# A new order of steps for a two-stage attention and token-mixing kernel, with batches 2 and 3 mixed in three pieces

## The chip, the cores and the metric

The kernel runs on one core of one Trainium2 chip. The metric is the time of one execution on the device in microseconds. The engines are named as the profile names them: PE (TensorE, the matmuls), PEld (its weight loads), DVE (VectorE), ACT (ScalarE), POOL (GpSimd) and SP (SyncE, used here only to issue DMAs). ACT and POOL can issue DMAs too.

## What is computed

Inputs q, k, v are of shape 8 batches x 8 heads x 576 tokens x 64, p is 8 x 8 x 32 x 64, all float32. The reference packs the tokens into 32 by an attention of p over k and v, and unpacks them by an attention of q over the packed tokens. The result, with heads side by side, is x (8 x 576 x 512), and goes through a mixing of tokens that is linear up to a relu:

```python
def sm_attn(qq, kk, vv):
    s = scale * np.matmul(qq, kk.transpose(0, 1, 3, 2))
    s = s - np.max(s, axis=-1, keepdims=True)
    a = np.exp(s)
    a = a / (np.sum(a, axis=-1, keepdims=True) + 1e-09)
    return np.matmul(a, vv)
p_packed = sm_attn(p, k, v)
out = sm_attn(q, p_packed, p_packed)
...
wq = x @ w_q
wk = x @ w_k
W_tok = scale * np.einsum('bsd,btd->bst', wq, wk)
mixed = np.einsum('bst,btd->bsd', W_tok, x)
return (np.maximum(mixed, 0.0) @ w_out).astype(np.float32)
```

## The kernel before

The work is cut by batch. Each batch b goes through the same steps, and each step is a small function whose name stands in a long string, ORDER. The loop at the end of the kernel walks through ORDER and emits one step after another, in a mode in which nothing reorders them: so ORDER is, for each engine and each DMA queue, the order of its work. Waits between engines follow from the data and the buffers. An item reads `NAME.batch.piece=banks@engine`; the banks are the PSUM banks that a matmul step writes, A, V, P and S are ACT, DVE, POOL and SP.

The steps of one batch, with the line at which the work is recorded where that isn't a shared helper:

- LD (loads). k, q and v come in over the POOL queue, and are cast from float32 to bf16 on the way; two halves of the batch's heads are two transfers for v always. In this kernel k is one transfer per batch (576 KB in bf16 counted as the profile does), but batch 0, whose first half comes as float32 over SP (LD.H, cast by HC) and whose second half is LD.g0. q is one transfer, but for batches 0 and 7 (LD.q and LD.r are its halves). LD.W, LD.O are weights, LD.P and LD.E parts of p. The order of LD items is the order in the POOL queue, where they stand among POOL's own work. Four buffers each hold k, q and v.
- KT, QV: k and q are transposed in 32 x 32 blocks on DVE (line 242); piece 0 or 1 is a half, piece 2 both halves in one instruction.
- S1 (line 278 for batches 0 and 1, line 288 for the others): scores of p over k. X1 (lines 296, 299): their exponential on ACT. TE (line 242): a transpose of it on DVE, for batches 2 to 7. PV (line 321): packed values and sums. RC, PP, PT (lines 325, 329, 242): reciprocal, normalisation, transpose, on DVE.
- QK, QKE, QD: the packed values by the two mixing weights, their eviction, a copy.
- S2 (line 379): scores of q over the packed tokens. X2 (line 384): their exponential. RS, RR, AM (lines 400, 405, 411): row sums, reciprocals and the product, which is the *mixing softmax*. RS and RR run on DVE, AM on DVE or POOL. AT (lines 420, 425): transposes on PE, AE: their eviction.
- WKQ (lines 447, 452), WE, GM (line 473), GE, Y (line 483), YE: the mixing, small matmuls each with an eviction. MX, MR (lines 498, 504) and RL, RLF, RLR (lines 509, 511): mixed tokens and their relu.
- OT (line 546), OH (line 583): the product with w_out; one piece is 128 tokens by 512, piece 4 the remaining tokens of two batches. OE, OEF, OEH: evictions on ACT or DVE (lines 127, 131). ST, STF, STH: stores, on the queues of SP, ACT and POOL. HOLD.v7 makes the SP queue wait for v of batch 7 before its first store.

A batch's 576 tokens are five blocks of 128, of which the last overlaps (line numbers of the profile's kernel). The steps from S2 to AE take them in the pieces of a table, `TCH = ((0, 2), (2, 4), (4, 5), (0, 4), (0, 5))`: pieces 0, 1 and 2 are three pieces of 2, 2 and 1 blocks; pieces 3 and 2 are two pieces of 4 and 1 blocks; piece 4 is all five. Batches 0, 1 and 7 go in three pieces, batches 2 to 6 in two, and those of 2 to 6 sum their rows in one instruction (RS.b.4).

WARM.n=bank is a filler: float32 matmuls over n x 128 columns into a bank that nobody reads (line 621); WARM.n.128 issues them 128 columns at a time, WARM.n 512 at a time. Each float32 matmul is two passes in the trace. Unlike other steps they compute nothing of the result.

The order of the first steps of before, and its steps around batch 7's S2:

```
SET.warm@V SET.v3@V SET.pz0@V LD.E0@A SET.tab@A SET.aT1@V LD.H@S LD.P3 LD.E1@S EC@A EX@V PB.0.1@V LD.g0
SET.v0@P HC@A PB.0.3@V PB.0.2@V KT.0.0@V KT.0.1@V LD.v0 PB.0.0@P WARM.4=0 WARM.16.128=0 S1.0=0,1,2 X1.0.0@A WARM.6=3
PV.0.0=4,5 PV.0.1 RC.0@V LD.q0 SET.mask@P SET.idf@V SET.aT0@V QV.0.1@V PP.0.0@V LD.P2 LD.r0 PP.0.1@V PT.0@V
SET.v2@V LD.W0 QV.0.0@V WARM.15=3 S2.0.2=6,7 LD.k1 LD.W1 SET.aT2@V LD.P1 KT.1.2@V S2.0.1=0,1 X2.0.1@A RS.0.1@V
...
RL.5.0@A GM.6=6 OT.5.4=7 RS.7.0@V RR.7.0@V GE.6@A S2.7.2=0,1 ST.2.1@P S2.7.1=4,5 X2.7.2@A QK.7=6 AM.7.0@P
```

Of the kernel before, what the change touches and what calls it, by code (L numbers as in the profile page):

```python
# [16 lines left out]
SET.v1@P S2.0.0=2,3 X2.0.0@A LD.v1 LD.P0 WARM.8=4 QK.0=4 RR.0.1@V AM.0.1@V QKE.0@A LD.q1 RS.0.0@V SET.aff@P
SET.idb@V WARM.3=5 S1.1=0,1,2 X1.1.0@A WARM.6=5 PV.1.0=4,5 PV.1.1 X2.0.2@A RR.0.0@V AT.0.1=3 AM.0.0@V AT.0.0=2
AE.0.0@A RC.1@V PP.1.1@V RS.0.2@V RR.0.2@V AM.0.2@V AE.0.1@A QD.0@A WARM.5=0 WKQ.0.0=0,1 AT.0.2=5 LD.k2
AE.0.2@A WARM.1=6 WKQ.0.2 LD.v2 WE.0.0@A WKQ.0.1 LD.q2 LD.k3 WE.0.1@A WARM.3=6 GM.0=5 PP.1.0@V PT.1@V QK.1=4  # L20
QV.1.2@V S2.1.1=6,7 GE.0@A S2.1.0=2,3 LD.O PX@V S2.1.2=0,1 KT.2.2@V QKE.1@A X2.1.1@A RS.1.1@V X2.1.0@A Y.0=4,5
YE.0@A WARM.1=6 S1.2=6,7,2,3 X2.1.2@A LD.v3 RS.1.0@V MX.0.1=4,5 RR.1.1@V X1.2.0@A TE.2.0@V X1.2.1@A TE.2.1@V
RR.1.0@V WARM.7=0 PV.2.0=0,1 PV.2.1 RL.0.1@A RS.1.2@V AM.1.0@V QD.1@A MR.0=6,7 RLR.0@A LD.k4 RR.1.2@V
MX.0.0=2,3 LD.q3 RC.2@V AT.1.0=4 AM.1.2@V AT.1.2=5 AE.1.2@A RL.0.0@A PP.2.1@V AM.1.1@P AT.1.1=6 AE.1.1@A
PP.2.0@V AE.1.0@V WARM.2=7 WKQ.1.0=0,1 WKQ.1.2 WARM.2=7 WKQ.1.1 QV.2.2@V WE.1.0@A PT.2@V S2.2.3=4,5 S2.2.2=2,3
KT.3.2@V WE.1.1@A GM.1=7 QK.2=6 GE.1@V WARM.3=0 Y.1=0,1 X2.2.2@A QKE.2@V S1.3=2,3,6,7 X2.2.3@A RS.2.4@V
RR.2.4@V LD.v4 X1.3.1@A TE.3.1@V X1.3.0@A TE.3.0@V OT.0.0=4,5 OT.0.1 LD.q4 YE.1@A AM.2.2@V OT.0.2=6,7 OE.0.0@V
OT.0.3 MR.1=2,3 OE.0.1@A RLR.1@V MX.1.1=0,1 PV.3.0=4,5 PV.3.1 RL.1.1@A RC.3@V PP.3.1@V PP.3.0@V KT.4.2@V
AM.2.3@P QD.2@P AT.2.3=2 AE.2.3@A OT.1.4=3 MX.1.0=6,7 AT.2.2=5 OEF.1.4@A AE.2.2@V WKQ.2.0=0,1 PT.3@V QV.3.2@V
WKQ.2.1 RL.1.0@A WKQ.2.2 WE.2.2@A S1.4=2,3,4,5 X1.4.1@A X1.4.0@A TE.4.1@V OT.1.0=6,7 LD.k5 GM.2=0 QK.3=1  # L30
QKE.3@A S2.3.2=4,5 X2.3.2@A S2.3.3=2,3 X2.3.3@A GE.2@V Y.2=0,1 OT.1.1 OE.1.0@A TE.4.0@V YE.2@V PV.4.0=4,5
PV.4.1 MX.2.0=0,1 RL.2.0@A RS.3.4@V LD.v5 RR.3.4@V RC.4@V LD.q5 PP.4.1@V PP.4.0@V PT.4@V OT.1.2=2,3 OT.1.3
QK.4=6 QV.4.2@V MX.2.1=0,1 MR.2=4,5 OE.1.1@A RL.2.1@A RLR.2@V AM.3.3@P QKE.4@V AT.3.3=7 AE.3.3@V QD.3@P
S2.4.2=2,3 X2.4.2@A LD.k6 KT.5.2@V S2.4.3=4,5 OT.2.2=0,1 X2.4.3@A QD.4@V RS.4.4@V RR.4.4@V AM.3.2@P AT.3.2=6
WKQ.3.0=2,3 WKQ.3.1 AE.3.2@A LD.v6 WKQ.3.2 WE.3.2@A S1.5=4,5,6,7 OT.2.3 X1.5.1@A TE.5.1@V GM.3=2 GE.3@V
OT.2.0=6,7 LD.q6 X1.5.0@A Y.3=4,5 TE.5.0@V PV.5.0=2,3 PV.5.1 OE.2.1@A YE.3@V MX.3.0=0,1 AM.4.2@P RC.5@V
PP.5.0@V AM.4.3@P PP.5.1@V RL.3.0@A MX.3.1=4,5 RL.3.1@V LD.k7 QV.5.2@V OT.2.1 OE.2.0@A LD.v7 AT.4.2=2 AE.4.2@A
AT.4.3=3 AE.4.3@A LD.r7 OT.3.0=0,1 MR.3=4,5 RLR.3@A LD.q7 OT.3.1 KT.6.2@V OE.3.0@A WKQ.4.0=6,7 WKQ.4.1 PT.5@V
WKQ.4.2 S1.6=2,3,4,5 OT.3.4=0 WE.4.2@V GM.4=1 X1.6.0@A TE.6.0@V S2.5.2=6,7 S2.5.3=2,3 X1.6.1@A TE.6.1@V
OEF.3.4@V GE.4@A X2.5.2@A HOLD.v7 Y.4=4,5 PV.6.0=6,7 X2.5.3@A ST.1.4 YE.4@V PV.6.1 RC.6@V PP.6.0@V QK.5=1  # L40
MX.4.0=4,5 PP.6.1@V ST.0.0 MX.4.1=2,3 QKE.5@A RL.4.0@A QV.6.2@V ST.1.1@P OT.3.2=0,1 OT.3.3 PT.6@V HA.5@P
# [18 lines left out]
def kernel(  # L60
# [89 lines left out]
    k_in = [const.tile([P, 2, RQ * Dh], bf16, name=f"k_sb{n}") for n in range(NL)]  # L150
    q_in = [const.tile([P, 2, RQ * Dh], bf16, name=f"q_sb{n}") for n in range(NL)]

    def load(x, eng):
        a, b = x[0], x[1:]
        if a == "g":
            nc.gpsimd.dma_start(k_in[0][:, 1], pairs(k, 0)[:, 1])
        elif a == "P":
            c = int(b)
            src = p.rearrange("b (i c) (y l) d -> c (b i) y (l d)", i=2, y=2)
            nc.gpsimd.dma_start(pbf[quarter(c)], src[c])  # L160
        elif a == "E":
            b = int(b)
            src = p[b].rearrange("(i c) l d -> (c l) i d", i=2)
            (nc.sync if eng == "S" else nc.scalar).dma_start(p32[:, 2 * b:2 * b + 2], src)
        elif a == "W":
            w = (moe_w_k, moe_w_q)[int(b)].rearrange("(i c j e) m -> (c j) i (e m)", i=2, c=4, e=2)
            nc.gpsimd.dma_start(wqk[:, :, int(b)].rearrange("a i e m -> a i (e m)"), w)
        elif a == "O":
            nc.gpsimd.dma_start(wout, moe_w_out.rearrange("(j a) n -> a j n", a=P))
        elif a == "H":  # L170
            nc.sync.dma_start(h32, pairs(k, 0)[:, 0])
        elif a == "v":
            b = int(b)
            for i in range(2):
                src = v[b, 4 * i:4 * i + 4].rearrange("c (g r) d -> g c (r d)", r=R)
                nc.gpsimd.dma_start(v_bufs[b % NL][halves(i), 0:7:2], src)  # L176
# [478 lines left out]
```

## Time and profile before

| what | us |
|---|---|
| three runs, median (lowest to highest) | 106.28 (105.72 to 106.77) |
| the profiled execution | 105.18 |
| its span, first to last instruction | 103.3 |
| granted PE clock, mean | 0.991 of full |

| engine | busy us | instructions |
|---|---|---|
| PE | 96.8 | 1544 |
| DVE | 75.7 | 150 |
| ACT | 66.2 | 109 |
| POOL | 49.9 | 76 |

The span is what the profile can see; some 1.9 us of the profiled execution lie outside it. Busy PE time includes the filler matmuls, and successive matmuls overlap in the records, since they are pipelined and their ends are modelled; a PE that is busy is therefore not a PE at its peak. A row of the timeline reads: start, duration, engine, source line, operation, output <- input, shapes, count, and in brackets the idle time of that engine ahead of it and what ended it. A row of the chain of waits reads: start, duration, what the end of the program depended on at that time. A group reads: line, engine, operation, shapes, count | busy us, mean ns of one | idle before, and who ended it. A window reads: stretch, its length, busy time of PE, PEld, DVE, ACT and POOL with the number of instructions, granted clock, DMA share, GB/s.

### The profile page before, as it was taken

What the parts mean: (1) busy time and instruction counts of PE and PEld (TensorE: products, weight loads), DVE (VectorE), ACT (ScalarE), POOL (GpSimd) and SP (SyncE); (2) the same over time, 40 slices, a digit from 0 to 9 for tenths busy, and PEclk for the clock granted to TensorE, in tenths of its full rate; (3) what the DMA queues carried; (4) which work ended last, traced back from release to release, by engine and by line L of the source; (5) the groups of instructions that cost most, each with busy time, mean ns of one, the idle gap of its engine ahead of it and who ended that gap; (6) DMA issues with size and microseconds to landing.
All of it is one profiled execution on the core that took longest, in us unless ns stands there. A gap on an engine that the chain in (4) does not pass through costs nothing.

```text
span 103.3 us, 3603 instructions
## 1 busy us (share of the span) xinstructions
PE 96.8 (94%) x1544; PEld 58.4 (57%) x1544; DVE 75.7 (73%) x150; ACT 66.2 (64%) x109; POOL 49.9 (48%) x76
## 2 busy tenths in 40 slices
...
GB/s 71 262 149 191 209 208 198 210 211 213 204 213 212 203 208 213 212 206 211 211 210 208 220 208 203 215 211 207 209 259 377 402 410 400 403 409 366 341 305 164
DMA packets 14079, 25.16 MB, mean 244 GB/s; under 512 B 2160, under 2 KB 7024, under 8 KB 14064
## 3 DMA queue, kind: packets, MB, share of 16 engines
...
HBM read 30.28 MB, written 9.44 MB: 384 GB/s over the span
## 4 chain that ended last, share of the span: by engine, by line
PE 73%; DVE 9%; DMA 5%; ACT 5%; POOL 3%; issue 2%; DVEq 0%; POOLq 0%; ACTq 0%
PE ps L546 25%; PE ps L621 13%; PE ps L321 6%; DMA k_sb<-in_k_dram 5%; PE ps L379 5%; PE ps L452 4%; PE ps L498 4%; PE ps L425 4%; DVE rs L400 3%; ACT e L384 3%; PE ps L447 3%; PE ps L278 2%; PE ps L473 2%; PE ps L288 2%; PE ps L342 2%; POOL a L411 2%
## 5 line engine op out<-in xcount | busy, mean ns | idle before, releaser
L546 PE MATMUL ps<-wout,relu 128*128 128x512 bf16 x124 | 30.5, 380 | 0.0
L411 POOL TENSOR_TENSOR a<-e,rr 128x1024 bf16<-128x1024 f32 (+2 forms) x13 | 15.6, 1211 | 19.1 <-DVE rr L405 11.0
L621 PE MATMUL ps<-o 128*128 128x128 f32 (+3 forms) x76 | 23.6, 452 | 1.3 <-DVE o L134 1.2
L127 ACT ACTIVATE o<-ps 128x1024 f32<-128x1024 f32 (+2 forms) x17 | 15.0, 888 | 6.9 <-PE ps L546 6.3
L546 PEld LDWEIGHTS <-relu 128*128 128x128 bf16 x124 | 10.7, 98 | 12.3 <-issue 1.8
L621 PEld LDWEIGHTS ps<-o 128*128 128x128 f32 x76 | 12.7, 220 | 7.1 <-issue 4.9
L384 ACT ACTIVATE e<-ps 128x256 f32<-128x256 f32 (+2 forms) x19 | 11.3, 621 | 5.9 <-PE ps L379 5.5
L509 ACT ACTIVATE relu<-ps 128x1024 bf16<-128x1024 f32 (+1 forms) x14 | 12.7, 933 | 2.2 <-PE ps L498 1.1
L242 DVE STREAM_TRANSPOSE kT<-k_sb 128x1152 uint32<-128x1152 uint32 (+1 forms) x9 | 11.1, 1232 | 3.0 <-DMA k_sb<-in_k_dram 2.9
L176 POOL DMA_DIRECT2D v_sb<-in_v_dram x16 | 10.1, 637 | 6.4 <-PE ps L425 2.1
L242 DVE STREAM_TRANSPOSE qT<-q_sb 128x1152 uint32<-128x1152 uint32 (+1 forms) x10 | 11.2, 1119 | 0.7 <-DMA q_sb<-in_q_dram 0.7
L400 DVE TENSOR_REDUCE rs<-e 128x16 f32<-128x512 f32 (+2 forms) x13 | 10.9, 846 | 0.5 <-ACT e L384 0.4
L321 PE MATMUL ps<-v_sb,e 64*64 64x192 bf16 x288 | 7.5, 245 | 0.7 <-DVE o L131 0.7
L299 ACT ACTIVATE e1T<-ps 128x576 bf16<-128x576 f32 x12 | 7.2, 663 | 1.3 <-PE ps L288 1.2
L127 ACT ACTIVATE aT<-ps 128x128 bf16<-128x128 f32 (+2 forms) x11 | 5.3, 506 | 3.6 <-PE ps L425 2.1
L321 PEld LDWEIGHTS <-e 64*64 64x64 bf16 x288 | 6.0, 107 | 2.6 <-issue 0.9
L127 ACT ACTIVATE wkq<-ps 128x448 bf16<-128x448 f32 (+1 forms) x9 | 6.3, 713 | 1.7 <-PE ps L452 1.4
L452 PE MATMUL ps<-aT,pqk 128*128 128x256 bf16 (+1 forms) x48 | 6.8, 246 | 0.1
L379 PEld LDWEIGHTS <-qT 64*128 64x128 bf16 x320 | 5.5, 94 | 2.3 <-issue 0.7
L379 PE MATMUL ps<-ppT,qT 64*128 64x64 bf16 x320 | 6.6, 190 | 0.0
L179 POOL DMA_DIRECT2D k_sb<-in_k_dram x7 | 5.2, 745 | 2.7 <-ACT g L127 2.7
L447 PE MATMUL ps<-pqk,aT 128*128 128x64 bf16 x80 | 6.1, 194 | 0.1
...
## 6 DMA issues: line engine op xcount, KB each, us to landing
...
```

The costliest lines, as they stand in the source:

```text
L127: nc.scalar.activation(o, i, COPY)
L176: nc.gpsimd.dma_start(v_bufs[b % NL][halves(i), 0:7:2], src)
L242: nc.vector.transpose(o, i)
L321: nc.tensor.matmul(T["pv", b][halves(cc), i], lhsT, rhs, start=n == 0, stop=n == R - 1, skip_group_check=True)
L379: nc.tensor.matmul(ps[:, y, t - t0, i], lhsT, rhs, start=e == 0, stop=e == 1)
L384: nc.scalar.activation(e2[:, t0:t1].rearrange("a t (i y n) -> a y (t i) n", i=2, y=2), T["s2", b, c].rearrange("a y t i n -> a y (t i) n") ...
L400: nc.vector.tensor_reduce(rs[:, t0 * H:t1 * H], src, axis=AX, op=ADD)
L411: e.tensor_tensor(a2[:, t0:t1].rearrange("a t i (u l) -> a (t i u) l", l=L), e2v(b, c), T["rr", b][:, t0 * H:t1 * H].to_broadcast((P, (t1 ...
L452: nc.tensor.matmul(o, pqk[:, i, Dl:], aT[:, i, c0:c1], start=i == 0, stop=i == 1)
L509: nc.scalar.activation(o, i, RELU)
L546: nc.tensor.matmul(ps, lhsT, wout[:, j, :], start=j == 0, stop=j == NJ - 1)
L621: nc.tensor.matmul(bank(int(bk), [w]), warm[:, 0:P], rhs, start=True, stop=True)
```

## The change

Three things change. First, two tables say of which batches k and q are loaded in halves (transfers and, in ORDER, transposes too): k of batches 1, 2 and 3 is now two transfers, LD.k (second half) and LD.j (first half); q of batches 0, 1, 2, 3 and 7 is LD.q and LD.r. The bytes are the same. Second, batches 2 and 3 take pieces 0, 1 and 2 from S2 to AE, where they took pieces 3 and 2 with one row sum over all. Third, ORDER is another one from its first item to its last: the same set of steps but for the pieces, with other places, in part other engines (HC from ACT to DVE, AM.6.3 from POOL to DVE, AE.5.3 and AE.6.3 from DVE to ACT, AM.2 all on POOL, for instance), other banks, and other fillers. Ahead of S1.0 WARM.4 and WARM.16.128 become WARM.20 and WARM.14.128; behind it 62 units become 34.

```diff
+QH, KH = (0, 1, 2, 3, 7), (1, 2, 3)
...
+LD.H@S LD.E0@A SET.warm@V SET.pz0@V SET.v0@V SET.idf@V LD.E1@S LD.W0 SET.aT2@V SET.tab@A EC@A EX@V PB.0.2@V
+HC@V LD.v0 KT.0.0@V LD.g0 PB.0.1@P PB.0.0@P KT.0.1@V PB.0.3@P WARM.20=0 WARM.14.128=0 S1.0=0,1,2 X1.0.0@A WARM.6=3
+PV.0.0=4,5 PV.0.1 SET.v1@V LD.q0 QV.0.1@V LD.r0 QV.0.0@V RC.0@V SET.aff@P SET.idb@V SET.mask@P PP.0.1@V LD.k1
+LD.j1 PP.0.0@V SET.v3@V PT.0@V WARM.8=3 S2.0.0=6,7 X2.0.0@A SET.aT0@V KT.1.0@V S2.0.2=0,1 X2.0.2@A S2.0.1=2,3
+X2.0.1@A KT.1.1@V RS.0.2@V RS.0.0@V WARM.3=5 S1.1=4,5,6 X1.1.0@A RR.0.0@V AM.0.0@V LD.r1 WARM.3=7 AT.0.0=7
+AE.0.0@A LD.W1 QK.0=0 QV.1.0@V LD.v1 WARM.2=1 PV.1.0=2,3 QKE.0@A RR.0.2@V LD.P3 RS.0.1@V RR.0.1@V AM.0.1@V
+PV.1.1 AM.0.2@V QD.0@V LD.q1 QV.1.1@V RC.1@V WARM.2=1 AT.0.2=1 AT.0.1=0 WKQ.0.0=4,5 AE.0.2@A WKQ.0.2 LD.P2
+AE.0.1@A PP.1.0@V PP.1.1@V LD.j3 WE.0.0@A LD.k2 SET.v2@V WKQ.0.1 WE.0.1@A WARM.2=6 GM.0=6 GE.0@A PT.1@V
+S2.1.1=0,1 X2.1.1@A Y.0=2,3 YE.0@V QK.1=7 QKE.1@A S2.1.0=4,5 LD.O MR.0=0,1 X2.1.0@A RS.1.1@V RR.1.1@V
+MX.0.1=2,3 LD.P1 LD.P0 RLR.0@A AM.1.1@V RS.1.0@V RR.1.0@V AM.1.0@V MX.0.0=6,7 RL.0.0@A RL.0.1@A S2.1.2=4,5
+WARM.6=0 OT.0.2=0,1 OT.0.3 LD.j2 AT.1.0=6 X2.1.2@A LD.k3 PX@V LD.r2 RS.1.2@V OE.0.1@A KT.2.1@V RR.1.2@V QD.1@V
...
+LD.r3 QV.2.1@V RL.1.1@A QK.2=5 LD.v4 TE.3.1@V WARM.1=2 S2.2.2=2,3 OEF.1.4@A S2.2.0=6,7 S2.2.1=0,1 QKE.2@A
+QD.2@A KT.4.2@V X2.2.2@A RS.2.2@V RR.2.2@V OT.1.0=4,5 OT.1.1 X2.2.1@A LD.q4 X2.2.0@A RS.2.0@V OE.1.0@A
+S1.4=2,3,0,1 RR.2.0@V LD.k5 PV.3.0=6,7 AM.2.2@P PV.3.1 X1.4.0@A RS.2.1@V RR.2.1@V AM.2.0@P AM.2.1@P AT.2.0=4
+RC.3@V PP.3.0@V PP.3.1@V X1.4.1@A TE.4.1@V QV.3.1@V AT.2.1=5 AE.2.0@A AE.2.1@A PT.3@V AT.2.2=2 AE.2.2@A LD.v5
+WKQ.2.0=0,1 WKQ.2.2 WE.2.0@A WKQ.2.1 QV.3.0@V S2.3.2=6,7 S2.3.0=4,5 WE.2.1@A X2.3.2@A TE.4.0@V X2.3.0@A GM.2=3
+S2.3.1=0,1 GE.2@A X2.3.1@A QK.3=2 QKE.3@A RS.3.2@V Y.2=6,7 RS.3.1@V RR.3.1@V YE.2@A PV.4.0=4,5 PV.4.1 MR.2=0,1
+RLR.2@A LD.k6 MX.2.0=2,3 MX.2.1=6,7 RL.2.0@A RS.3.0@V RR.3.0@V AM.3.1@P RL.2.1@A OT.1.2=0,1 OT.1.3 RR.3.2@V
...
+RL.4.0@A QV.6.2@V S2.6.2=2,3 S2.6.3=6,7 OT.4.0=0,1 OT.4.1 HA.5@P RS.5.4@V RR.5.4@V OE.3.1@A X2.6.2@A ST.3.1
+ST.1.4@P X2.6.3@A ST.0.0 OE.4.0@A QK.6=4 QKE.6@A KT.7.2@V S1.7=2,3,6,7 RS.6.4@V X1.7.1@A RR.6.4@V TE.7.1@V
+AM.5.3@P AT.5.3=5 AE.5.3@A OT.4.2=0,1 OT.4.3 AM.5.2@P AM.6.3@V QD.6@P AT.5.2=4 AE.5.2@V X1.7.0@A TE.7.0@V
+OE.4.1@A QD.5@P WKQ.5.0=6,7 ST.1.0 WKQ.5.1 ST.4.1 QV.7.0@V AT.6.3=5 WKQ.5.2 PV.7.0=2,3 QV.7.1@V ST.2.1@P
+PV.7.1 RC.7@V AM.6.2@P AT.6.2=4 AE.6.3@A WKQ.6.0=0,1 ST.3.0 WKQ.6.1 WE.5.2@A AE.6.2@V WKQ.6.2 PP.7.1@V ST.0.1
+WE.6.2@A ST.3.4@P PP.7.0@V PT.7@V GM.5=5 S2.7.0=6,7 X2.7.0@A S2.7.1=2,3 GE.5@V Y.5=4,5 YE.5@V QK.7=0 QKE.7@V
+X2.7.1@A ST.2.0 RS.7.1@V RR.7.1@V GM.6=1 S2.7.2=6,7 GE.6@A MR.5=4,5 ST.4.0 QD.7@V X2.7.2@A MX.5.0=2,3 Y.6=0,1
+RLR.5@A MX.5.1=6,7 RL.5.1@V OT.5.4=4 YE.6@A MX.6.1=0,1 RL.5.0@A AM.7.1@P OEF.5.4@A MX.6.0=2,3 RL.6.0@A
+RS.7.0@V RR.7.0@V AM.7.0@V AT.7.1=5 OT.5.2=6,7 OT.5.3 RS.7.2@V RL.6.1@A OT.6.0=2,3 RR.7.2@V AM.7.2@V AT.7.2=4
...
     def load(x, eng):
         a, b = x[0], x[1:]
...
-        elif a == "k":
+        elif a == "g":
+            nc.gpsimd.dma_start(k_in[0][:, 1], pairs(k, 0)[:, 1])
+        else:
             b = int(b)
-            nc.gpsimd.dma_start(k_in[b % NL], pairs(k, b))
-        elif a == "r" or x in ("q0", "q7"):
-            b, i = int(b), int(a == "q")
-            nc.gpsimd.dma_start(q_in[b % NL][:, i], pairs(q, b)[:, i])
-        else:
-            b = int(b)
-            nc.gpsimd.dma_start(q_in[b % NL], pairs(q, b))
+            t, src, half = (k_in, k, KH) if a in "jk" else (q_in, q, QH)
+            if b in half:
+                i = int(a in "kq")
+                nc.gpsimd.dma_start(t[b % NL][:, i], pairs(src, b)[:, i])
+            else:
+                nc.gpsimd.dma_start(t[b % NL], pairs(src, b))
```

The table and the longer ORDER move all later lines by two or three: line 278 of before is 280 of after, line 400 is 402, line 411 is 413, line 546 is 548 and line 621 is 623.

65 lines of the change are left out of this document (19 added, 46 removed).

## The prediction

> **What bounds the kernel now.** I read the engine shares and the chain of waits first, then the chain in order of time, then the DMA by windows. First the shares of the page, and its chain:
>
> ```profile
> PE 96.8 (94%) x1544; PEld 58.4 (57%) x1544; DVE 75.7 (73%) x150; ACT 66.2 (64%) x109; POOL 49.9 (48%) x76
> PE 73%; DVE 9%; DMA 5%; ACT 5%; POOL 3%; issue 2%; DVEq 0%; POOLq 0%; ACTq 0%
> ```
>
> TensorE (PE) looks full, with 6.5 us idle in a span of 103.3. But part of "full" is filler (the WARM matmuls of line 621). The timeline's row for the second half of k0, and the chain behind it, show how they alternate with real work:
>
> ```profile
> 7.61 0.78 DVE L242 STREAM_TRANSPOSE kT<-k_sb 128x576 uint32<-128x576 uint32 x1 [0.32 <-DMA k_sb<-in_k_dram]
> ```
> ```profile
> 8.44 1.23 PE ps L278 x35
> 9.67 1.49 PE ps L621 x4
> 11.16 0.87 PE ps L321 x36
> 12.02 3.42 PE ps L621 x8
> ```
>
> The first scores (S1.0, line 278) start at 8.44, as soon as the second half of k is transposed. The 3.42 us are WARM.15: 0.228 us per unit of 128 columns. Behind S1.0 the order has 62 such units, 14.1 us that stand where TensorE would otherwise wait. The second bound is the DMA:
>
> ```profile
> 74.00:76.00 2.00, 2.00 (x50) 1.01 (x49) 1.97 (x3) 2.00 (x3) 2.00 (x3) 1.00 1.13 212
> ...
> 86.00:88.00 2.00, 2.00 (x16) 0.90 (x13) 1.87 (x4) 1.49 (x2) 1.80 (x3) 1.00 1.02 399
> ```
>
> The last two columns are the DMA's share and rate. Loads (which cast to bf16) run as a conveyor at some 210 GB/s until the last q arrives, stores at 400 after it. Neither the bytes nor the packets change, so batch 7's inputs can't come much sooner.
>
> **The change, part by part.** *Start.* In the POOL queue one 64 KB load and both halves of v0 now stand ahead of the second half of k0 (LD.g0); before, one 64 KB load did. When v0 was issued, how long its two halves took, and the narrow fillers ahead of S1.0 in 0 to 5 us and in 6.1 to 8:
>
> ```profile
> 3.48 1.24 POOL L176 DMA_DIRECT2D v_sb<-in_v_dram x2 [0.30 <-POOL v_sb L209]
> ```
> ```profile
> DMA to landing us min/median/max: 6.0/6.4/6.9
> ```
> ```profile
> L621 PE MATMUL ps<-o 128*128 128x128 f32 x10 | 2.3, 421 | 0.0
> ```
> ```profile
> L621 PE MATMUL ps<-o 128*128 128x128 f32 x19 | 2.3, 278 | 0.0
> ```
>
> The last of v0, issued some 0.6 into that row, at 4.1, landed 6.9 later, at 11.0. k0's second half takes that place in the conveyor, and is issued up to 0.8 sooner, since no memset stands between: 10.2 to 11.0; I take 10.4. With the transpose of 0.78, S1.0 starts at 11.2: **+2.8 us** (2.6 to 3.4). The fillers ahead of it are now 10 passes of 512 columns and 28 of 128. The two rows give 0.22 us for 128 columns early (2.3 over 10) and 0.12 late (2.3 over 19), with the change of rate between 5 and 6.1: five or six wide ones slow to there, four or five at half that to 8.0, 28 × 0.11 behind them: they end near 11.0, under the wait for k.
>
> *Fillers.* Behind S1.0 34 units remain of 62: 28 × 0.228 = **-6.4 us**, if nothing waits instead.
>
> *Pieces and halves.* Their prices, from the groups by shape on VectorE, on POOL and on ScalarE:
>
> ```profile
> L242 DVE STREAM_TRANSPOSE kT<-k_sb 128x1152 uint32<-128x1152 uint32 x7 | 9.5, 1361 | 2.7 <-DMA k_sb<-in_k_dram 2.6
> ...
> L400 DVE TENSOR_REDUCE rs<-e 128x40 f32<-128x1280 f32 x4 | 5.9, 1469 | 0.5 <-ACT e L384 0.4
> ...
> L400 DVE TENSOR_REDUCE rs<-e 128x16 f32<-128x512 f32 x6 | 3.9, 658 | 0.0
> ...
> L242 DVE STREAM_TRANSPOSE qT<-q_sb 128x576 uint32<-128x576 uint32 x4 | 3.0, 755 | 0.2 <-DMA q_sb<-in_q_dram 0.2
> L411 DVE TENSOR_TENSOR a<-e,rr 128x256 bf16<-128x256 f32 x3 | 2.6, 854 | 0.0
> L242 DVE STREAM_TRANSPOSE ppT<-pp 128x128 uint32<-128x128 uint32 x8 | 2.3, 292 | 0.1
> L411 DVE TENSOR_TENSOR a<-e,rr 128x512 bf16<-128x512 f32 x3 | 2.1, 687 | 0.1
> L131 DVE COPY aT<-ps 128x1024 bf16<-128x1024 bf16 x3 | 2.1, 685 | 0.1
> ```
> ```profile
> L411 POOL TENSOR_TENSOR a<-e,rr 128x512 bf16<-128x512 f32 x3 | 3.1, 1041 | 4.6 <-DVE rr L405 4.6
> L411 POOL TENSOR_TENSOR a<-e,rr 128x256 bf16<-128x256 f32 x5 | 3.1, 618 | 1.4 <-DVE rr L405 1.3
> ```
> ```profile
> L509 ACT ACTIVATE relu<-ps 128x1024 bf16<-128x1024 f32 x11 | 11.1, 1022 | 2.2 <-PE ps L498 1.1 <-DVE rr L405 1.0
> L384 ACT ACTIVATE e<-ps 128x512 f32<-128x512 f32 x6 | 3.4, 594 | 5.1 <-PE ps L379 5.1
> ```
>
> Per batch, reductions of 0.66, 0.66 and (estimate, by size) 0.39 replace one of 1.47, and two reciprocals more come with them: about +0.5 us of VectorE. Two half transposes of 0.755 take 1.51 against 1.36 for a whole, six times; the six more loads of half the size are issued by POOL, which is idle half the span. Against that a 512-wide piece is ready 0.59 + 0.66 + 1.04, with its reciprocal about 2.5 us after its scores, where the whole took over four. None of this is on TensorE; what counts is whether it makes TensorE wait where fillers stood. I walked the new order engine by engine with durations of this trace (where several of a kind follow each other, start to start: exponentials of 512 0.55, relu and evictions of 1024 0.95). Four places come out with TensorE idle:
> - From RC.0 to PT.1 VectorE runs 27 instructions without a break, about 10.2 us (two half q, two half k, three reductions, three products, four PP, two memsets of 0.45). They end at 25.2, so S2.1 starts about two us sooner than before, but TensorE waits some 0.4 for the products.
> - Then ScalarE runs without a break from the exponentials of batch 1 to OE.1.0 near 44; OT.0.2 waits 0.5 for RL.0.1.
> - POOL multiplies all three pieces of batch 2: 0.62 + 2 × 1.04 = 2.7 us, from 43.0 to 46.05. Behind PV.3 TensorE has only AT.2 and WKQ.2 (1.3 us of work) until 47.7: over 2 us idle, the largest hole. LD.v5 and LD.k6 stand behind these products in POOL's queue; before, LD.k6 stood behind AM.3.3 in the same way.
> - Batch 3's pieces: 0.7.
>
> Less what stood idle before on the same work, that is **+2.6 us** (1.0 to 4.5: the low end if POOL starts when VectorE's first reciprocal is there 1 us sooner, the high end if the ScalarE stretch slips by 2). To OT.4.1, where both orders have done exactly the same work, the sum is 2.8 - 6.4 + 2.6 = -1.0. Before ended that step here:
>
> ```profile
> 73.16 1.88 PE ps L546 x8
> 75.04 0.34 PE ps L342 x8
> ```
>
> *Batch 7.* This lead isn't kept. S2.7.0 needs PT.7, which ends a run of VectorE's queue, and in before the two met within 0.1 us:
>
> ```profile
> 74.51 1.44 DVE L400 TENSOR_REDUCE rs<-e 128x40 f32<-128x1280 f32 x1
> ...
> 78.60 0.78 DVE L242 STREAM_TRANSPOSE qT<-q_sb 128x576 uint32<-128x576 uint32 x1 [0.24 <-DMA q_sb<-in_q_dram]
> ...
> 81.55 0.31 DVE L242 STREAM_TRANSPOSE ppT<-pp 128x128 uint32<-128x128 uint32 x1
> ```
> ```profile
> 81.95 0.38 PE ps L379 x16
> ```
>
> From RS.6.4 (74.51) to the end of PT.7 before took 7.35 us. In the new order this queue loses two evictions of 0.69 (to ScalarE) and 0.7 of idle, and gains AM.6.3 on VectorE, 128x1024: by twice the 0.69 of a 512 at most 1.4, I take 1.2 (estimate), and two short evictions (0.5, estimate). That makes 7.0. RS.6.4 waits for ScalarE (X2.6.3 behind a relu and an eviction) and starts near 74.15. S2.7.0 then starts near 81.25: **0.7 sooner** than before. The last q isn't late: it is used at 79, and landed at 78.6 before.
>
> *Tail.* The new order has Y.5, MR.5 and MX.5.1 (0.46 us together) still to do behind S2.7.0, and waits of some 0.3 us (OT.6.0 for RL.6.1, OT.7.2 for the last relu on ScalarE). The end itself is the same, two half output steps, their evictions, stores and landing; before, TensorE ended at 99.5, 3.8 us ahead of the span's end:
>
> ```profile
> 98.60 0.89 PE ps L583 x8
> ```
>
> So -0.7 + 0.46 + 0.3 = +0.1 us on the span of 103.3.
>
> [...] VectorE and POOL collided once:
>
> ```profile
> 40.16 1.73 DVE L411 TENSOR_TENSOR a<-e,rr 128x256 bf16<-128x256 f32 x1
> ```
> ```profile
> 39.70 1.90 POOL L411 TENSOR_TENSOR a<-e,rr 128x1024 bf16<-128x1024 f32 x1 [3.11 <-DVE rr L405]
> ```
>
> 256 columns took 1.73 us while POOL ran its own product; the other two of that shape share the rest of the 2.6 us, 0.42 each. [...]
>
> In the new order AM.2 has no such collision (1.3 less, in the walk above). AM.6.3 meets AM.6.2 on POOL; by my walk VectorE is there first (76.5 against 76.8), and POOL's wait is hidden. HC, now on VectorE and not ScalarE, costs 0.7 to 1.6 (the 128x1024 copy above took 0.69, two half transposes of as many elements 1.5); it lies under the 2.4 us for which k0's second half is still awaited.
>
> **The rivals.** (1) *The fillers' time is kept.* If the pieces reach POOL earlier than I walked, the extra idle is 1.0 and the lead at OT.4.1 2.6; VectorE then starts RS.6.4 1.6 sooner, S2.7.0 can start at 80.2 with the last q landing by 78.6, and the end is 1.7 sooner: 104.7. For it: fillers are the only work removed. Against: ScalarE and VectorE are packed there.
> (2) *AM.6.3 is blocked* (slower). If POOL's AM.5.3, AM.5.2 and copies run later than 76.5, VectorE waits as at 40.16: 1.3 us, straight into PT.7, S2.7.0 and everything behind it: 106.4 + 1.3 = 107.7. It decides once AM.5.3 starts later than about 74.0; I have 72.75.
> (3) *The fillers come back as waits.* If nothing of the 6.4 is saved, the later start remains, +2.8: 109.1. For it: the filler stood where data was late. Against: S2.1 and the normalisation of batch 0 are ready sooner by the walk.
> That the change doesn't do what it says I give nothing: each piece is its own instruction on each engine.
>
> **How the numbers follow.** The profiled run of before took 105.18 us for its span of 103.3; the median of the others is 106.28, 1.1 above. +0.1 gives **106.4**. One per cent, about what a measurement tells from no change, is 1.06 us. Forecast, within that: 0.44. Rival 1: 0.26. Rival 2: 0.18. Rival 3: 0.12. So faster 0.26, same 0.44, slower 0.30. The forecast's own range is 105.3 to 107.4; down to 104.6 it takes in rival 1 as priced, up to 108.3 rival 2 and half of rival 3.
>
> **What would show it.** Right: S1.0 (line 280 after) starts near 11.2; TensorE idle of some 2 us between the PV of batch 3 and WKQ.2, waiting for POOL; OT.4.1 ends near 74; S2.7.0 near 81.3. Wrong: S1.0 below 10 or above 12, no hole at batch 2, a VectorE product of 128x1024 well over 1.3 us, or a tail in which stores and not matmuls end last.

## The result, and the profile of the changed kernel

| | before | changed |
|---|---|---|
| median of 22 runs each (lowest to highest), us | 105.78 (105.34 to 106.77) | 106.67 (105.82 to 107.83) |
| ratio to before, 95% interval | | 1.0072 [1.0045, 1.0099] |
| the profiled execution, us | 105.18 | 107.09 |
| its span, us | 103.3 | 105.2 |

The changed kernel is 0.7% slower, a small loss but clear of no change, and within the one per cent called "same"; forecast were 106.4 us and a range of 104.6 to 108.3. The profiled execution of before lies 0.6 us below its median and that of the changed kernel 0.4 above, so the 1.9 us between the two spans overstate the change by about one. Ratios here and below leave out executions more than 1.5% slower than the fastest of the same kernel.

Engine shares of the changed kernel's page, and its chain of waits:

```profile
PE 94.6 (90%) x1532; PEld 56.5 (54%) x1532; DVE 75.3 (72%) x163; ACT 69.8 (66%) x121; POOL 48.7 (46%) x79
...
PE 56%; DMA 17%; ACT 11%; DVE 8%; issue 3%; POOL 2%; DVEq 0%; ACTq 0%
```

TensorE is idle for 10.6 us of the span, before for 6.5. In the chain DMA has grown from 5% to 17%, at the cost of PE: by its rows it now runs through the load of k0's second half (7.28 us) and that of v of batch 1 (10.22 us), where it ran through matmuls, fillers among them. Where this begins is in POOL's timeline, which holds the loads it issues, first of before (q0), then of the changed kernel:

```profile
5.73 0.44 POOL L129 COPY o<-o 32x256 bf16<-32x256 bf16 x1 [1.00 <-DVE o L242]
6.12 0.55 POOL L182 DMA_DIRECT2D q_sb<-in_q_dram x1
```
```profile
2.60 1.24 POOL L177 DMA_DIRECT2D v_sb<-in_v_dram x2 [0.47 <-DVE aT L137]
3.83 0.58 POOL L179 DMA_DIRECT2D k_sb<-in_k_dram x1
5.82 1.75 POOL L132 COPY o<-o 32x256 bf16<-32x256 bf16 x3 [1.41 <-DVE o L244]
7.52 1.09 POOL L185 DMA_DIRECT2D q_sb<-in_q_dram x2
```

The load of v0 waited 0.47 us for a memset on VectorE (the row names that of aT; the ones of v0's buffer are set in the same queue shortly before, 1.76 to 2.30). Then POOL stands idle for 1.41 us and makes three copies for 1.75 (PB.0.1, PB.0.0, PB.0.3), and only then, from 7.52, issues q0; before made one copy there and issued q0 at 6.12. VectorE shows what that does:

```profile
11.13 0.78 DVE L244 STREAM_TRANSPOSE kT<-k_sb 128x576 uint32<-128x576 uint32 x1 [3.44 <-DMA k_sb<-in_k_dram]
...
14.09 0.78 DVE L244 STREAM_TRANSPOSE qT<-q_sb 128x576 uint32<-128x576 uint32 x1 [1.57 <-DMA q_sb<-in_q_dram]
15.47 0.78 DVE L244 STREAM_TRANSPOSE qT<-q_sb 128x576 uint32<-128x576 uint32 x1 [0.60 <-DMA q_sb<-in_q_dram]
```

The second half of k0 is used at 11.13, the first half of q0 2.96 later, though the two halves of q0 are 1.38 apart (14.09 and 15.47). TensorE at the same time, at OT.4.1 and at S2.7.0:

```profile
11.96 1.24 PE L280 MATMUL ps<-o,kT 128*64 128x128 bf16 x35 [1.29 <-DVE kT L244]
...
17.86 0.78 PE L381 MATMUL ps<-ppT,qT 64*128 64x64 bf16 x40 [0.39 <-DVE aT L137]
...
74.28 1.90 PE L548 MATMUL ps<-wout,relu 128*128 128x512 bf16 x8
...
82.91 0.66 PE L381 MATMUL ps<-ppT,qT 64*128 64x64 bf16 x32
```

S1.0 runs at 11.96 (8.44 before), OT.4.1 ends at 76.18 (75.04 before), S2.7.0 starts at 82.91 (81.95 before). So of the 1.9 us that this execution is longer, 1.1 are there at OT.4.1 and 1.0 at S2.7.0; the tail behind S2.7.0 adds the rest. VectorE and POOL around batch 7:

```profile
74.60 1.40 DVE L244 STREAM_TRANSPOSE kT<-k_sb 128x1152 uint32<-128x1152 uint32 x1 [0.37 <-DMA k_sb<-in_k_dram]
75.92 1.49 DVE L402 TENSOR_REDUCE rs<-e 128x40 f32<-128x1280 f32 x1
...
78.49 1.35 DVE L413 TENSOR_TENSOR a<-e,rr 128x1024 bf16<-128x1024 f32 x1
...
80.36 1.39 DVE L244 STREAM_TRANSPOSE qT<-q_sb 128x576 uint32<-128x576 uint32 x2
...
82.55 0.31 DVE L244 STREAM_TRANSPOSE ppT<-pp 128x128 uint32<-128x128 uint32 x1
```
```profile
78.70 1.61 POOL L413 TENSOR_TENSOR a<-e,rr 128x256 bf16<-128x256 f32 x1
```

KT.7.2 at 74.60 waits 0.37 us for k of batch 7, so here a load, and not ScalarE, holds this queue. The two transposes of the last q show no wait: they start at 80.36, as the step before them ends. From RS.6.4 (75.92) to the end of PT.7 are 6.94 us. AM.6.3 takes 1.35 us, starts first, and POOL's AM.6.2 beside it takes 1.61. Last, TensorE behind PV.3, where AT.2 and WKQ.2 stand:

```profile
47.06 0.40 PE L427 MATMUL ps<-idb,a 128*128 128x128 bf16 x4 [0.19 <-POOL a L413]
48.07 0.40 PE L427 MATMUL ps<-idb,a 128*128 128x128 bf16 x4 [0.61 <-POOL a L413]
...
49.32 0.23 PE L449 MATMUL ps<-pqk,aT 128*128 128x64 bf16 x2 [0.47 <-ACT aT L130]
```

Here it waits for POOL's products twice and once for an eviction on ScalarE, 1.27 us in all.

### The profile page after: what moved, and what is told of

The parts are those of the page before. It is cut to its first block, busy times and chain, and to the rows that moved or that the text cites. A ratio compares the mean times of both kernels' runs of the same rounds, so it can differ in the third digit from the quotient of the medians.

```text
span 105.2 us, 3594 instructions
## 1 busy us (share of the span) xinstructions
PE 94.6 (90%) x1532; PEld 56.5 (54%) x1532; DVE 75.3 (72%) x163; ACT 69.8 (66%) x121; POOL 48.7 (46%) x79
## 4 chain that ended last, share of the span: by engine, by line
PE 56%; DMA 17%; ACT 11%; DVE 8%; issue 3%; POOL 2%; DVEq 0%; ACTq 0%
PE ps L548 27%; DMA v_sb<-in_v_dram 10%; DMA k_sb<-in_k_dram 7%; PE ps L323 5%; PE ps L381 4%; PE ps L500 3%; PE ps L427 3%; PE ps L623 2%; ACT e L386 2%; PE ps L454 2%; DVE kT L244 2%; ACT o L130 2%; PE ps L449 2%; PE ps L475 2%; POOL v_sb L177 2%
## 5 line engine op out<-in xcount | busy, mean ns | idle before, releaser
L623 PE MATMUL ps<-o 128*128 128x128 f32 (+3 forms) x64 | 19.2, 437 | 1.2 <-DVE o L137 1.2
L413 POOL TENSOR_TENSOR a<-e,rr 128x256 bf16<-128x256 f32 (+2 forms) x12 | 12.9, 1091 | 12.8 <-ACT y L492 4.9
L386 ACT ACTIVATE e<-ps 128x512 f32<-128x512 f32 (+2 forms) x21 | 11.4, 580 | 6.5 <-PE ps L381 6.2
L244 DVE STREAM_TRANSPOSE kT<-k_sb 128x576 uint32<-128x576 uint32 (+1 forms) x12 | 11.5, 970 | 4.4 <-DMA k_sb<-in_k_dram 4.4
L511 ACT ACTIVATE relu<-ps 128x1024 bf16<-128x1024 f32 (+1 forms) x16 | 14.6, 949 | 0.0
L244 DVE STREAM_TRANSPOSE qT<-q_sb 128x576 uint32<-128x576 uint32 (+1 forms) x13 | 11.6, 899 | 3.5 <-DMA q_sb<-in_q_dram 3.4
L623 PEld LDWEIGHTS ps<-o 128*128 128x128 f32 x64 | 9.9, 201 | 6.8 <-issue 4.8
L130 ACT ACTIVATE aT<-ps 128x512 bf16<-128x512 bf16 (+2 forms) x11 | 6.3, 588 | 3.2 <-PE ps L422 2.4
L298 ACT ACTIVATE e<-ps 128x1152 bf16<-128x1152 f32 x2 | 2.3, 1131 | 9.2 <-PE ps L280 9.2
L185 POOL DMA_DIRECT2D q_sb<-in_q_dram x10 | 5.5, 554 | 4.9 <-DMA q_sb<-in_q_dram 2.2
```

The source lines that it names most:

```text
L130: nc.scalar.activation(o, i, COPY)
L244: nc.vector.transpose(o, i)
L386: nc.scalar.activation(e2[:, t0:t1].rearrange("a t (i y n) -> a y (t i) n", i=2, y=2), T["s2", b, c].rearrange("a y t i n -> a y (t i) n") ...
L413: e.tensor_tensor(a2[:, t0:t1].rearrange("a t i (u l) -> a (t i u) l", l=L), e2v(b, c), T["rr", b][:, t0 * H:t1 * H].to_broadcast((P, (t1 ...
L511: nc.scalar.activation(o, i, RELU)
L623: nc.tensor.matmul(bank(int(bk), [w]), warm[:, 0:P], rhs, start=True, stop=True)
```

## The experiments

Each kernel is the changed kernel with one edit unless it says "before". All were timed in five rounds, on several chips, each beside runs of before on its own chip, from which its ratio comes.

**q0 ahead of POOL's copies.** LD.q0 and LD.r0 stand right behind LD.g0.

```diff
-HC@V LD.v0 KT.0.0@V LD.g0 PB.0.1@P PB.0.0@P ... PV.0.1 SET.v1@V LD.q0 QV.0.1@V LD.r0
+HC@V LD.v0 KT.0.0@V LD.g0 LD.q0 LD.r0 PB.0.1@P PB.0.0@P ... PV.0.1 SET.v1@V QV.0.1@V
```

> The changed kernel with LD.q0 and LD.r0 issued by POOL right behind LD.g0, ahead of the three PB copies, and nothing else. Theory L (late loads: in the changed kernel q0 landed 2.96 us behind the second half of k0 instead of 1.4, because the three copies of 1.75 us stand ahead of its issue, and every later load and all work fed by it slid by that): q0 lands by 12.6, the last q by 79.5 instead of 80.8, S2.7.0 starts 1.2 to 1.6 us sooner than 82.9, ratio to the kernel before 0.990 to 0.997 where the changed kernel has 1.007. Theory P (the pieces and POOL's products at batch 2 are what costs): no change, 1.004 to 1.010.

Ratio 0.9969 [0.9928, 1.0009], one per cent better than the changed kernel's 1.0072. S1.0 still waits as long for k0 (VectorE waits 3.64 us for its second half, 3.44 in the changed kernel). The loads between 10 and 20 us, in the windows of before, of the changed kernel and of this one (stretch, then busy time by engine, and at the end granted clock, DMA share and GB/s):

```profile
10.00:20.00 10.00, 10.00 (x130) 5.25 (x130) 5.42 (x16) 2.31 (x4) 7.15 (x13) 1.00 1.19 206
```
```profile
10.00:20.00 10.00, 8.21 (x136) 4.94 (x136) 6.17 (x16) 2.49 (x4) 5.53 (x10) 1.00 1.13 189
```
```profile
10.00:20.00 10.00, 9.16 (x165) 6.02 (x164) 7.03 (x17) 2.50 (x4) 5.62 (x10) 1.00 1.16 206
```

189 GB/s against 206 over 10 us are some 0.8 us of the conveyor, the stream of loads, lost (17 of 206, times 10). From 30 to 70 us both load at the same rate (209, 209, 211 and 210 GB/s over ten us each in the changed kernel, 208, 209, 211 and 210 here), so nothing makes that up. S2.7.0 starts at 81.82 here, 1.1 us sooner than in the changed kernel, a little less than the first theory said:

```profile
81.82 0.66 PE L381 MATMUL ps<-ppT,qT 64*128 64x64 bf16 x32
```

**Two pieces again.** Batches 2 and 3 take pieces 3 and 2 with one row sum, at the places that the new order gives to the three (batch 2 is shown, batch 3 is alike).

```diff
-S2.2.2=2,3 ... S2.2.0=6,7 S2.2.1=0,1 ... AM.2.2@P ... AM.2.0@P AM.2.1@P
+S2.2.2=2,3 ... S2.2.3=6,7 ... RS.2.4@V ... AM.2.2@P ... AM.2.3@P
```

> The changed kernel with batches 2 and 3 back at two pieces (one row sum and one reciprocal over all, products of 1024 and 256 on POOL), in the places of the new order; the halves stay. Theory L: the pieces help or do nothing, so without them the hole behind PV.3 grows by 0.5 to 1.5 us, ratio 1.007 to 1.020. Theory P: the hole shrinks, ratio at most 1.002.

Ratio 1.0447 [1.0390, 1.0504]. TensorE, where batch 2 is awaited, and the granted clock there:

```profile
47.40 0.75 PE L425 MATMUL ps<-idb,a 128*128 128x128 bf16 x8 [1.90 <-POOL a L411]
```
```profile
42.00:46.00 4.00, 2.92 (x74) 1.00 1.15 209
46.00:50.00 4.00, 1.59 (x18) 0.72 1.19 211
50.00:54.00 4.00, 3.92 (x88) 0.50 1.11 211
54.00:58.00 4.00, 3.77 (x54) 0.93 1.18 210
```

The pieces don't hurt, as one theory had it; in this order they are worth 3.7%, more than either theory said. Without them TensorE waits 1.90 us behind PV.3, the granted clock is 0.72 from 46 to 50 us and 0.50 in the next four, and the matmuls there take up to 1.6 times as long (S2.3 takes 1.25 us, S2.0 in the changed kernel, with the clock at 1.00, 0.78). All six runs of this kernel had a mean clock of 0.968 or 0.969. So the 3.7% are the hole and the clock together.

**AM.6.3 on POOL**, as before.

```diff
-AM.5.2@P AM.6.3@V QD.6@P
+AM.5.2@P AM.6.3@P QD.6@P
```

> The changed kernel with the product AM.6.3 on POOL and not on VectorE. Theory L: VectorE's queue up to PT.7 is released by the last q anyway (landed 80.83, its transpose followed at once), so that 1.35 us less ahead of it gain at most 0.3: ratio 1.004 to 1.010. Theory C (the product on VectorE, and its collision with POOL's AM.6.2, which took 1.61 us and not 0.62, hold up batch 7): 0.7 to 1.3 us faster, ratio 0.995 to 1.001.

Ratio 1.0234 [1.0186, 1.0283], so the move to VectorE is worth 1.6%; neither theory had it. TensorE's wait is not for AM.6.3 but for the copy QD.6, which stands behind it in POOL's queue:

```profile
PE ps L454 <- POOL pqk L132: 1.1, 1, 1.1
```
```profile
78.84 1.91 POOL L413 TENSOR_TENSOR a<-e,rr 128x1024 bf16<-128x1024 f32 x1 [1.10 <-DVE rr L407]
80.70 0.52 POOL L132 COPY pqk<-pqk 128x128 bf16<-128x128 bf16 x2
```

From the end of OT.4.1 (77.01) to S2.7.0 (84.85) this execution takes 7.84 us, the changed kernel 6.73: that wait is what the edit costs at S2.7.0, 1.1 us. Up to OT.4.1 it lost 0.8 us more, ahead of the edit: its clock was 0.92 at 46 to 50 us and 0.65 at 50 to 54 (1.00 in the changed kernel), and its mean of 0.984 is the lowest of the six.

**k and q of batches 1 to 3 whole.**

```diff
-QH, KH = (0, 1, 2, 3, 7), (1, 2, 3)
+QH, KH = (0, 7), ()
-LD.k1 LD.j1 PP.0.0@V ... KT.1.0@V ... KT.1.1@V
+LD.k1 PP.0.0@V ... KT.1.2@V
```

> The changed kernel with k and q of batches 1 to 3 loaded whole, where the second of the two halves stood, and transposed whole, where the later half stood; the three pieces stay. Theory L: the conveyor is as late as before, the transposes of batches 1 to 3 start later and block VectorE: ratio 1.007 to 1.020. Theory H (the halves cost, by six more transposes and six more issues on POOL): ratio at most 1.003.

Ratio 1.0159 [1.0120, 1.0197]: the halves are worth 0.9%, about as the first theory said, and theory H falls. TensorE waits for VectorE's transposes by 0.66, 0.33 and 0.43 us, at S2.1, S1.3 and S2.2, where the rows of the changed kernel show no wait.

**The changed kernel again.**

> The changed kernel once more, beside the others on one chip. Theory L (what the new order loses, it loses at the start; q of batch 0 stands behind POOL's three copies, and lands at another time in each execution): ratio 1.004 to 1.011, S1.0 near 12, q of batch 0 anywhere from 12.2 to 14.1, and the end of the span moves with it. Rival (the late q0 of the first profile was a single accident): q0 lands near 12.3, the last q near 79.3, ratio at or below 1.004.

Ratio 1.0132 [1.0078, 1.0186]; the first theory allowed up to 1.011. VectorE:

```profile
13.48 0.78 DVE L244 STREAM_TRANSPOSE qT<-q_sb 128x576 uint32<-128x576 uint32 x1 [1.00 <-DMA q_sb<-in_q_dram]
```

The late q0 is no accident: 13.48 here, 14.09 in the first profile, and 12.65, right behind another instruction, where it was issued early. S1.0 starts at 11.92, OT.4.1 ends at 75.62 and S2.7.0 starts at 82.36. One program thus gave 1.0072 and 1.0132, each with an interval that holds 1.0078 to 1.0099, so what an edit is worth is known to some half a per cent only. Against 1.0132 the pieces are worth 3.1%, the move of AM.6.3 1.0%, moving q0 1.6%, and the halves 0.3%, which is within the noise.

**An early start.** In POOL's queue k0's second half comes first, then v0 (its ones set sooner), then q0, then the copies; the weight load moves behind k1; the fillers ahead of S1.0 are those of before.

```diff
-SET.warm@V SET.pz0@V SET.v0@V SET.idf@V LD.E1@S LD.W0 SET.aT2@V ... LD.j1 PP.0.0@V
+SET.warm@V SET.v0@V SET.pz0@V SET.idf@V LD.E1@S LD.g0 LD.v0 LD.q0 LD.r0 SET.aT2@V ... LD.j1 LD.W0 PP.0.0@V
-WARM.20=0 WARM.14.128=0 S1.0=0,1,2
+WARM.4=0 WARM.16.128=0 S1.0=0,1,2
```

> The changed kernel with k0's second half first in POOL's queue, then v0 (its ones set first by VectorE), then both halves of q0, then POOL's copies; the 64 KB weight load behind k1; the fillers ahead of S1.0 as in the kernel before. Theory L: S1.0 starts near 8.5 instead of 12, the lead reaches S2.1 and is kept until the waits of batches 2 and 3, and the time falls below that of the edit which only moved q0 (0.997): ratio 0.985 to 0.992. Rival C (the conveyor of loads sets the place of everything behind it, and the start of S1.0 is of no account, since TensorE then waits for q, k and VectorE): S1.0 near 8.5 but S2.7.0 within 0.3 us of that edit's 81.8, ratio 0.994 to 1.000.

Ratio 0.9954 [0.9917, 0.9992]. TensorE:

```profile
8.28 1.44 PE L280 MATMUL ps<-o,kT 128*64 128x128 bf16 x36
...
15.65 0.79 PE L381 MATMUL ps<-ppT,qT 64*128 64x64 bf16 x40 [1.67 <-DVE aT L137]
...
50.21 0.93 PE L323 MATMUL ps<-v_sb,e 64*64 64x192 bf16 x35 [0.87 <-DMA v_sb<-in_v_dram]
...
54.97 0.78 PE L381 MATMUL ps<-ppT,qT 64*128 64x64 bf16 x40
...
72.94 1.90 PE L548 MATMUL ps<-wout,relu 128*128 128x512 bf16 x8
...
81.57 0.66 PE L381 MATMUL ps<-ppT,qT 64*128 64x64 bf16 x32
```

S1.0 is some 3.5 us sooner than in the changed kernel, but S2.7.0 only 0.25 sooner than where q0 alone was moved (81.82). The lead goes into waits: for q0 and the packed values ahead of S2.0 (1.67), for v ahead of PV.4 (0.87). The rival that the start of S1.0 is of no account fits, and the theory that the lead is kept (0.985 to 0.992) falls. The same kernel on another chip:

> The early start once more, on another chip than its first run (0.995 there; the version that has PV of batch 4 moved as well gave 1.005 elsewhere). If the early start stands level with the kernel before, and chips and executions scatter by half a per cent around it: ratio 0.993 to 1.003. If it is really faster: below 0.997 with the whole interval below 1. If the first run was luck, and the moved PV changes nothing: 1.003 to 1.007. In the profile, S2.4 between 54.9 and 55.5 and S2.7.0 between 81.4 and 82 in each case, though S1.0 starts some 3.6 us before that of the changed kernel.

Ratio 0.9999 [0.9963, 1.0035]. Level with before, then, and not shown to be faster. Its profiled execution, the slowest of twelve (107.59 us), has S2.4 at 56.82 and S2.7.0 at 83.32, later than expected, and shows one thing that can hold such an order back:

```profile
14.00:18.00 4.00, 2.04 (x44) 0.93 1.25 199
18.00:22.00 4.00, 3.66 (x39) 0.50 1.17 209
22.00:26.00 4.00, 4.00 (x63) 0.72 1.15 210
```

The time won at S1.0 is time in which TensorE has nothing to do at 14 to 18 us (busy for 2.04 of 4 here), and in some executions the clock falls: 6 of the 12 had a mean clock between 0.968 and 0.979. Among those that the ratio counts, the four with such a clock have a median of 106.26 us, the six others 105.57.

**The early start, with PV.4 later.** As that kernel, and PV.4 behind the mixing products of batch 2, with an output step of batch 1 ahead of them.

```diff
-Y.2=6,7 ... PV.4.0=4,5 PV.4.1 MR.2=0,1 ... MX.2.1=6,7 ... OT.1.2=0,1 OT.1.3
+Y.2=6,7 OT.1.2=0,1 ... MR.2=4,5 ... MX.2.1=6,7 PV.4.0=4,5 PV.4.1 ... OT.1.3
```

> The early start as run before (0.995), and PV of batch 4 moved behind the mixing products of batch 2, with one output step of batch 1 ahead of them, so that TensorE works while v of batch 4 is awaited (MR.2 in other banks for it). Theory P4 (TensorE's waits up to about 54 us set the end, because it is full behind them): the 0.87 us wait for v goes, S2.4 starts 0.3 to 0.5 us sooner, ratio 0.989 to 0.993. Rival C (the loads set the places of batches 4 to 7 whatever stands between them): S2.7.0 as before this edit, within 0.2 us of 81.6, ratio 0.994 to 0.998.

Ratio 1.0046 [1.0013, 1.0079]; the theory of TensorE's waits falls. Rival C has the places right (S2.7.0 at 81.41), but its ratio is missed too. The wait for v ahead of PV.4 is gone, and S2.4 starts where it did:

```profile
51.60 0.94 PE L323 MATMUL ps<-v_sb,e 64*64 64x192 bf16 x36
...
55.01 0.78 PE L381 MATMUL ps<-ppT,qT 64*128 64x64 bf16 x40
```

**No fillers behind S1.0**, in the changed kernel: all 34 units taken out.

> The changed kernel without the 34 filler units behind S1.0 (7.8 us of matmuls that nobody reads). Theory L (fillers only stand where TensorE would wait anyway, and the clock stays up): ratio to before 1.003 to 1.010, as the changed kernel, and TensorE's busy time falls by some 7.5 us while its idle time grows by as much. Rival K (fillers keep the granted clock up): the mean granted clock falls, matmuls of the first 30 us take up to twice as long, ratio 1.02 or more. Rival W (the fillers are themselves in the way): ratio 0.97 to 0.99.

Ratio 1.0082 [1.0036, 1.0128]. Its twelve runs spread widely: the median of all is 107.38 against 107.06 of the changed kernel on the same chip (six runs), and the highest 109.47 against 108.08. The clock did fall, in every run (means of 0.947 to 0.984), as rival K said, but the 2% that it asked for did not come. The profiled execution by windows:

```profile
10.00:20.00 10.00, 6.01 (x140) 5.12 (x140) 6.77 (x16) 2.49 (x4) 5.47 (x10) 0.82 1.11 186
20.00:30.00 10.00, 9.14 (x167) 6.78 (x161) 7.24 (x20) 5.81 (x13) 5.19 (x9) 0.67 1.16 209
30.00:40.00 10.00, 7.63 (x138) 3.91 (x135) 8.87 (x21) 8.16 (x15) 5.15 (x9) 1.00 1.14 209
```

The slow matmuls seem to fill time in which TensorE would have waited (it is busy for 9.14 of 10 us at 20 to 30, at a clock of 0.67), and cost little.

**No fillers behind S1.0 in before**: all 62 units taken out.

> The kernel before without its 62 filler units behind S1.0 (14.1 us of matmuls that nobody reads). Theory W (in both orders the fillers stand only where TensorE waits for loads and for VectorE, so their removal saves nothing and their number is no measure of what an order can win): ratio 0.995 to 1.01, TensorE's idle time 13 to 15 us higher, PV of batch 4 within 0.6 us of 50.7. Theory F (what the prediction reckoned with: filler time is mostly gained where fillers go): the time falls by at least 3 us, ratio 0.97 or less. If the granted clock falls as it did without the fillers of the changed kernel, theory W allows up to 1.01, since the slow stretch would lie in front of data that is late anyway.

Ratio 1.0426 [1.0388, 1.0464]: slower, which neither theory had.

```profile
10.00:20.00 10.00, 3.61 (x101) 3.09 (x102) 5.28 (x15) 2.60 (x4) 7.21 (x13) 0.66 1.19 205
20.00:30.00 10.00, 7.05 (x104) 5.41 (x102) 7.73 (x16) 4.20 (x9) 4.21 (x7) 0.50 1.14 210
30.00:40.00 10.00, 8.38 (x154) 5.24 (x150) 6.93 (x17) 6.96 (x15) 3.21 (x5) 0.50 1.17 208
40.00:50.00 10.00, 8.69 (x163) 5.04 (x164) 8.22 (x14) 5.82 (x9) 5.01 (x6) 0.97 1.15 211
```

The clock stays at half for some 27 us (estimate, from the 0.66, 0.50, 0.50 and 0.97 of these windows, counted as time at 0.50 and at 1.00). The edit takes out nothing but fillers, so the slower matmuls are the likeliest cause of the loss: what was slack becomes the path. Filler time is no reserve that an order could draw on at will: in the order before the clock is at 1.00 in each of these windows with the fillers, and without them it falls.

**The late k0 alone, in before.** Its second half behind v0 in POOL's queue.

```diff
-LD.g0 SET.v0@P HC@A PB.0.3@V PB.0.2@V KT.0.0@V KT.0.1@V LD.v0
+SET.v0@P LD.v0 LD.g0 HC@A PB.0.3@V PB.0.2@V KT.0.0@V KT.0.1@V
```

> The kernel before with one edit: k0's second half stands behind v0 in POOL's queue, as in the changed kernel. Theory L: S1.0 moves from 8.4 to 11 or 12, nothing behind it can make up for it since TensorE has its fillers still to do, and the time rises by 2 to 3 us: ratio 1.018 to 1.03. Rival C (the conveyor sets the place of everything): S1.0 moves as much, but the first data after it is no later than before, ratio at most 1.008.

Ratio 1.0321 [1.0255, 1.0387]. The short fillers ahead of S1.0 end long before k0 is there; in the profiled execution (111.49 us, the highest of its runs) TensorE stands idle for 4.12 us, and S1.0 takes 2.13 us, not 1.24 (granted clock 0.66 over 10 to 20 us):

```profile
11.99 2.13 PE L278 MATMUL ps<-o,kT 128*64 128x128 bf16 x35 [4.12 <-DVE kT L242]
```

So the same edit again, with the fillers of the changed kernel ahead of S1.0:

```diff
-WARM.4=0 WARM.16.128=0 S1.0=0,1,2
+WARM.20=0 WARM.14.128=0 S1.0=0,1,2
```

> The kernel before with k0's second half behind v0, and with the fillers ahead of S1.0 as in the changed kernel, so that TensorE does not stand idle while it waits. Theory D (the delay of S1.0 itself passes through, since 62 filler units still follow it): S1.0 near 11.5, granted clock full throughout, ratio 1.022 to 1.032, nearly the 1.032 of the unfilled edit. Rival K (most of that loss was the granted clock at half after the idle stretch): ratio 1.005 to 1.018.

```profile
12.14 1.24 PE L278 MATMUL ps<-o,kT 128*64 128x128 bf16 x35 [0.74 <-DVE kT L242]
```

Ratio 1.0274 [1.0238, 1.0311], clock 0.992 or more in every run. In the old order a start 3.7 us later costs 2.9 us in the medians: most of it passes through. Theory D holds, and so does the first theory of the unfilled edit, whose 1.0321 lies just above its range.

## Why the prediction was right, and where only its sum was

The forecast (+0.1 us on the span, "same") held: +0.9 us between the medians. That it held was partly luck. Up to OT.4.1 the sum was wrong by 2.1 us, and two of the signs that were named for being right were missed: OT.4.1 ended at 76.18 and not near 74, and S2.7.0 started at 82.91 and not near 81.3. The 106.4 also started from a median of three runs, 106.28, which stands at 105.78 with 22: half a microsecond of its closeness to 106.67 is chance. The sum to OT.4.1, by TensorE's busy time in each profile from the start of S1.0 to the end of OT.4.1 (the granted clock is 1.00 in all three):

| us | before | changed | early start |
|---|---|---|---|
| S1.0 starts | 8.44 | 11.96 | 8.28 |
| fillers | 16.57 | 9.88 | 9.95 |
| all other matmuls | 48.67 | 50.35 | 50.69 |
| TensorE idle | 1.36 | 3.99 | 5.92 |
| OT.4.1 ends | 75.04 | 76.18 | 74.84 |

Records of neighbours overlap (in the changed kernel S1.0 ends at 13.20 and the filler behind it starts at 13.13), so the split between fillers and the rest is rough to a few tenths.

- *Start, +2.8.* As a delay it was sized too low: S1.0 came 3.5 us later, outside the 2.6 to 3.4 given, in part since v0's load did wait for a memset (on VectorE, 0.47 us), against "no memset stands between"; k0 was used at 11.13 where 10.4 was taken for its landing. As a cost it belongs to the order. In the old one such a delay costs 2.9 us (late k0, filled); in the new one taking it away again saved 0.25 us at S2.7.0 and nothing certain in the ratio (0.9954 and 0.9999, against 0.9969).
- *Fillers, -6.4, and extra idle, +2.6.* In the changed kernel both came out as forecast, -6.7 and +2.6. What the sum has at nothing is that the other matmuls take 1.7 us longer, those of S2 and PV 0.7 and 0.5 over the whole span (7.3 against 6.6, 8.0 against 7.5); why is not shown. With the start, 3.5 - 6.7 + 2.6 + 1.7 = +1.1, where -1.0 was forecast.
- *Adding the terms.* This is the step that failed. With the start of before, as in the early start, the terms ask for an OT.4.1 at 75.04 - 6.4 + 2.6 = 71.2; it ended at 74.84. There 4.6 us came back as idle time and 2.0 as longer matmuls, all of what the fillers freed: the third rival's mechanism. (The profile of before is 0.6 us below its own median, that of the early start at its median, so some half a microsecond may have been kept.) It wasn't slower by that rival's price, because most of the late start stands in the same waits. The terms for start, fillers and idle aren't to be added: with S1.0 3.5 us sooner TensorE waited later for other inputs (1.67 us ahead of S2.0, 0.87 ahead of PV.4).
- *The hole at batch 2.* It is there, waiting for POOL and then ScalarE, as said, but smaller: 0.19 + 0.61 + 0.47 = 1.27 us where over 2 were forecast.
- *Batch 7.* The last q landed at some 80.8, where the old order had it at 78.6, but "the last q isn't late" holds in that nothing waited for it. The queue as a whole came later: RS.6.4 started at 75.92 against 74.15, behind an OT.4.1 that was 2.1 us later than forecast and a wait of 0.37 us for k of batch 7. POOL's three copies ahead of LD.q0 weren't costed at all, though the prediction weighs just that for LD.v5 and LD.k6: the conveyor lost 0.8 us there, and moving LD.q0 alone regained 1.0%. The walk of VectorE's queue was right, 7.0 us forecast and 6.94 measured. In the early start RS.6.4 waits 0.41 us for ScalarE, as the prediction has it, and S2.7.0 came at 81.57, against 81.25.
- *Tail, +0.46 and +0.3.* Right as a sum: from S2.7.0 to the last matmul before took 17.52 us (81.95 to 99.47), the changed kernel 18.26 (82.91 to 101.17).
- *The collision of AM.6.3 and AM.6.2.* VectorE was first, 78.49 against 78.70, with 1.35 us where 1.2 was taken, and POOL's AM.6.2 beside it took 1.61 against its usual 0.62; TensorE came to AT.6.2 only at 81.44, so that was hidden, and the second rival didn't come about. At 40.16 in before it was VectorE that started second and took longer, 1.73 against 0.42. With AM.6.3 moved back to POOL, AM.6.2 took 0.63 us. Why the second of the two takes longer is not shown. What AM.6.3 on VectorE was worth wasn't priced: it keeps QD.6 from standing behind a product of 1.9 us on POOL.

So the change is not one edit that costs 0.7%. In the new order pieces (3.1 to 3.7%) and the moved product (1.0 to 1.6%) help, against the order without them, the halves (0.3 to 0.9%) don't hurt, and q0 behind POOL's copies takes 1.0 to 1.6% back. Why the early start, without that fault, is only level with before stays open: waits ahead of S2.0 and PV.4 (1.67 and 0.87 us) and the falling clock (106.26 against 105.57 us) take part of its lead, but with the wait at PV.4 gone no time was won.
